# Freeing eight splits, moving the first weight sums behind block 1's routing, and adding an unread exponential

## The chip, the cores and the metric

The kernel runs on one core of a Trainium2 chip. The metric is device time in microseconds (us); lower is better. The engines are TensorE (PE, with its weight loads as PEld), VectorE (DVE), ScalarE (ACT), GpSimd (POOL) and SyncE (SP), which here only issues transfers. Each has its own queue of instructions and they meet through semaphores.

## The reference

Three stages follow one another: an attention with two local masks, a gated layer, and a soft mixture of experts. Cut to what matters here:

```python
attn_out = _attn_ref(q, k, v)                     # 4 x 8 x 576 x 64
x = attn_out.transpose(0, 2, 1, 3).reshape(2304, 512)
gate = 1.0 / (1.0 + np.exp(-(x @ w_gate)))        # w_gate, w_val: 512 x 1536
x = (gate * (x @ w_val)) @ w_out                  # w_out: 1536 x 512
logits = x @ phi                                  # 2304 x 32
d = softmax(logits, axis=0); c = softmax(logits, axis=1)
slot_input = d.T @ x                              # 32 slots, 4 for each of 8 experts
h = np.maximum(slot_input[e] @ w1[e], 0.0); slot_out[e] = h @ w2[e]
out = c @ slot_out
```

## The kernel before

The 2304 tokens are cut into five blocks: blocks 0 to 3 have 512 tokens, block 4 has 256. The work around the change is the passage from block 1 to the pair of blocks 2 and 3.

**Block 1** (`l1`, called for twelve column groups f of the gated layer) makes two groups of twelve matmuls for each f, one for the gate (ScalarE applies the sigmoid, L537) and one for the value (VectorE multiplies, L539). Every fp32 operand is split into a high part, a cast on ScalarE, and a low part, a subtraction. Between the groups, other work is put in: the attention scores, their transposes (tile `tr`, copied by ScalarE to `pt_ring`, L189), the weighted sums (`xp`, L208) of the blocks to come, and the routing of block 0.

**The routing** of a block is class `Post`: `logits` (PSUM tile `lt_ps`, then a running maximum and two exponentials on ScalarE, L805 and L809), twelve `turn` steps (four PE transposes each into a tile `tp`, copied to `gt` by ScalarE at L826 or VectorE at L824), `weights` (`dt_ps`) and three `gather` products (`sp`, added to `acc`, L862 and L864). For block 1 all copies to `gt` are ScalarE's.

**The pair** of blocks 2 and 3 (`pair_l1`, twelve f) uses a scheme of seven products of 2 by 2 blocks in place of eight. It wants differences of the tokens: `pair_sums` makes four of them on POOL (tile `tsum`, eight instructions at L577, steps 0 to 3 of two halves each). `pair_t` splits them into `t1` (from step 0), `t2` (step 2), `t3` (step 1) and `t4` (step 3): eight casts on ScalarE at L553 and eight subtractions on VectorE at L554 (tile `t_hl`). `pair_x2` and `pair_x3` split the tokens themselves (`b_hi`, `b_lo`, `b22`). It also wants sums of the weights of each f (class `PairW`, tile `s`, made by VectorE at L613) and their splits: `high0`, `high1`, `high2` are casts on ScalarE (L627, L630/L631, L641), `low0` is VectorE's, `low1` and `low2` are POOL's. `first_w`, `first_sums` and `first_splits` do that for f = 0. The products are at L651: `pa` (PSUM of the first, second, third and the last, in turn), `pd` and `pe`.

**What sets the order.** A scheduler places every instruction by its own estimate of times, except those given to `keep_in_program_order` (by `kept`, or by `kp` while `fixed[0]` is set; the helper `pinned` sets it around a call): these stay in the order in which they are written. Before the change all of `pair_sums` and `pair_t` are pinned and written ahead of block 1's routing, and `first_sums` and `first_splits` are the last two of the steps that `Spread` deals out between the routing's steps. PSUM tiles `tr`, `tp`, `pd` and `pe` share four banks (pool `ps_a`): the transposes of a new tile wait until the tile that had the bank is copied out. `xp`, `sp` and `lt_ps` share two (`ps_m`).

Of the kernel before, what the change touches and what calls it, by code (L numbers as in the profile page):

```python
# [7 lines left out]
F32 = mybir.dt.float32  # L8
# [4 lines left out]
AF = mybir.ActivationFunctionType  # L13
# [4 lines left out]
P = 128  # L18
# [4 lines left out]
NF = 12  # L23
# [32 lines left out]
def pb_tokens(n):  # L56
    return 512 if n < 4 else 256
# [3 lines left out]
def tile_kernel(  # L61
# [10 lines left out]
    nc = tc.nc  # L72

    cpool = ctx.enter_context(tc.tile_pool(name="cpool", bufs=1))
# [12 lines left out]
    def b8(tag, shape, dt, name):  # L87
        return big.tile(shape, dt, tag=tag, name=name, bufs=BUFS[tag])
# [28 lines left out]
    for i in range(SMALL):  # L117
        g = slice(32 * (i % 4), 32 * (i % 4) + 32)
# [392 lines left out]

    g_sb = {}
    g_cur = {}

    def l1(n, f, whl, between):
        nt = pb_tokens(n)
        per = 2048 // nt
        tag = {0: "ga", 1: "gb", 4: "xt" if f < per else "xb"}[n]
        if (n, f // per) not in g_cur:
            g_cur[n, f // per] = b8(tag, [P, per, nt], F32, "g")  # L520
        g = g_cur[n, f // per][:, f % per]
        for a in range(2):
            pt = ps_l1.tile([P, 512], F32, tag="l1", name="l1ps")
            first = True
            for dc in HP_ORDER:
                for w_, x_ in ((0, x_hi), (0, x_lo), (1, x_hi)):
                    nc.tensor.matmul(  # L527
                        pt[:, 0:nt],
                        lhsT=whl[:, w_, a, dc, :],
                        rhs=x_[n][:, dc, :],  # L530
                        start=first,
                        stop=(dc == HP_ORDER[-1] and w_ == 1),
                    )
                    first = False
            with tc.high_priority(offset=HIP):
                if a == 0:
                    nc.scalar.activation(g, pt[:, 0:nt], AF.Sigmoid)  # L537
                else:
                    nc.vector.tensor_tensor(g, pt[:, 0:nt], g, ALU.mult)  # L539
            between()  # L540
        g_sb[n, f] = g
# [10 lines left out]
    def split(eng, hi, lo, src_):  # L552
        kp(nc.scalar.copy(hi, src_))  # L553
        kp(eng.tensor_tensor(lo, src_, hi.bitcast(F32), ALU.subtract))  # L554
# [31 lines left out]
    def pair_t(z, c):  # L586
        name, at = (("t1", (0, 0)), ("t2", (2, 0)), ("t3", (0, 1)), ("t4", (2, 1)))[z]
        if c == 0:
            t = b8(("qk", "v")[z % 2], [P, 2, 2, 512], F32R, "t_hl")
            pair[name] = t[:, 0], t[:, 1]  # L590
        hi, lo = pair[name]
        split(nc.vector, hi[:, c], lo[:, c], pair["t", at[0]][:, at[1], c])
# [380 lines left out]
    for f in range(NF):  # L973
        whl = split_w(conv.pop(f), SPL)
        ahead(f + LA)
        if f >= 10:
            store()
            load_w(f - 10)
        l1(0, f, whl, sab if f < wo_first else ticking)
        if f in wo_at:  # L980
            convert(NF + wo_at[f])
# [10 lines left out]
    for f in range(NF):  # L992
        whl = split_w(wst[f // 2][:, f % 2])
        if f % 2:
            load_w(f // 2 + 2)
        l1(1, f, whl, beside)
        if NF + f in wo_at:
            convert(NF + wo_at[NF + f])
# [21 lines left out]
        prev_w[0].high2()  # L1020
        prev_w[0].low2()

    early_prep = [(pair_sums, z) for z in range(4)] + [(pair_t, z, c) for z in range(4) for c in range(2)]
    prep = [(pair_x2, z) for z in range(4)]
    prep += [(first_w,), (pair_x3, 0), (pair_x3, 1), (first_sums,), (first_splits,)]

    def pinned(fn, *args):
        fixed[0] = True
        fn(*args)
        fixed[0] = False  # L1030

    for x in early_prep:
        pinned(*x)
    prep = [(pinned, *x) for x in prep]
    after = after[mix0.done :] + Post(1).all()
    mix = Spread(prep, [(len(after) - 3, len(prep))])
    for fn, *args in after:
        fn(*args)
        mix()
    prev = None  # L1040
    w4 = []

# [26 lines left out]
    for f in range(NF):  # L1069
        l1(4, f, split_w(w4[f // 2][:, f % 2]), mix)  # L1070
        if f % 2:
            load_w4()
        for n, tags in ((n2, ["ga"] * 3), (len(after), ["gb"] * 3 + ["l2"] * 2)):
            if done < n <= mix.done:
                room += tags
                load_e(len(room))
        done = mix.done
        if f == NF - 2:
            load_wo("ws")
# [20 lines left out]
    for f in range(NF):  # L1100
        c = f % 4
# [18 lines left out]
    for e in range(8):  # L1120
        for h in range(2):
# [8 lines left out]
            tag = reuse.pop(0) if reuse else None  # L1130
# [226 lines left out]
```

## Time and profile before

| | us |
|---|---|
| median of three runs | 498.23 (497.89 to 499.33) |
| profiled execution, its own time | 498.77 |
| span of its core | 496.8 |
| PE busy | 470.1 (95%) |
| DVE busy | 301.4 (61%) |
| ACT busy | 248.6 (50%) |
| POOL busy | 158.3 (32%) |

The span is what the trace covers; 2 us of the execution lie around it. A row of the timeline has the start in us from the span's start, the duration, the engine, the line and the operation, the tile written and those read, the shape and the count; in brackets stands how long the engine was idle before and what released it. A row with a count merges neighbours, and rows of different engines, or of PE's overlapping matmuls, can overlap. Ends of matmuls are modelled.

### The profile page before, as it was taken

Reading aid. Unit: us, or ns where it says so; the run is one execution under the profiler, and the core shown is the slowest. Engines: PE = TensorE matmul, PEld = TensorE weight load, DVE = VectorE, ACT = ScalarE, POOL = GpSimd, SP = SyncE. Lnnn points to the kernel's source line nnn. Section 1 sums busy time; section 2 is a strip of 40 time slices with the busy share of each in tenths; the row PEclk is TensorE's granted clock in tenths of the full one; section 3 lists DMA queues with packets and bytes.
Section 4 is the critical chain, followed back from the end, with each engine's and each line's share of the span. In section 5 each row is a group of like instructions: output and inputs, shape, how many; then the busy total and the mean of one; then the engine's idle time right before and its main releaser. Section 6 shows DMA issues by size and latency. Waiting matters only on the chain.

```text
span 496.8 us, 12732 instructions
## 1 busy us (share of the span) xinstructions
PE 470.1 (95%) x5476; PEld 357.7 (72%) x5476; DVE 301.4 (61%) x561; ACT 248.6 (50%) x428; POOL 158.3 (32%) x132
## 2 busy tenths in 40 slices
PE   6789999999899999999889999999999999999993
PEld 3468877878677877877458888888887889643552
DVE  3969698967767353555956566556557665521522
ACT  2466566747666453546855545545435544300232
POOL 0243555635383321182143243342312134010100
PEclk9989999999999999999989999999999999989998
DMA  8979898979986501750020220220699795679997
GB/s 327 405 258 335 290 369 305 322 270 364 408 289 211 172 3 49 253 195 3 0 84 2 84 86 1 86 84 0 239 383 424 288 341 191 251 257 367 421 392 219
DMA packets 23784, 112.13 MB, mean 226 GB/s; under 512 B 2352, under 2 KB 7216, under 8 KB 14640
## 3 DMA queue, kind: packets, MB, share of 16 engines
q1 hardware_dynamic: 23408, 111.06, 60.1%
q8 instruction: 43, 0.70, 0.6%
q10 hardware_dynamic: 320, 0.26, 0.2%
q14 instruction: 13, 0.11, 0.1%
HBM read 97.16 MB, written 14.16 MB: 224 GB/s over the span
## 4 chain that ended last, share of the span: by engine, by line
PE 76%; DVE 3%; ACT 3%; issue 2%; DMA 1%; POOL 1%; SPq 0%; ACTq 0%; DVEq 0%; POOLq 0%
PE l1ps L527 27%; PE pa L651 13%; PE pe L651 6%; PE tp L821 4%; PE h_ps L1123 3%; PE pd L651 3%; PE xp L208 3%; PE so_ps L1182 2%; PE sp L852 2%; PE lt_ps L785 2%; PE s_ps L145 2%; PE wt_ps L468 1%; PE tr L188 1%; PE op L1221 1%; PE si_ps L1102 1%
## 5 line engine op out<-in xcount | busy, mean ns | idle before, releaser
L527 PE MATMUL l1ps<-x_hi,whl 128*128 128x512 f32 x384 | 129.5, 404 | 3.1 <-ACT x_hi L229 2.3
L527 PEld LDWEIGHTS l1ps<-x_hi,whl 128*128 128x128 f32 x384 | 72.2, 189 | 20.4 <-ACT x_hi L229 3.0
L527 PE MATMUL l1ps<-x_lo,whl 128*128 128x512 f32 x192 | 76.1, 397 | 0.0
L442 POOL TENSOR_TENSOR fw<-fw 128x512 int32<-128x512 int32 x36 | 51.4, 1437 | 71.5 <-DVE fw L441 35.1
L527 PEld LDWEIGHTS l1ps<-x_lo,whl 128*128 128x128 f32 x192 | 36.4, 190 | 7.2 <-issue 0.4
L539 DVE TENSOR_TENSOR g<-l1ps,g 128x512 f32<-128x512 f32 (+1 forms) x36 | 21.6, 600 | 32.7 <-PE l1ps L527 32.2
L527 PE MATMUL l1ps<-x,whl 128*128 128x256 f32 x288 | 37.2, 286 | 0.0
L527 PEld LDWEIGHTS l1ps<-x,whl 128*128 128x128 f32 x288 | 35.4, 191 | 2.1 <-issue 1.9
L537 ACT ACTIVATE g<-l1ps 128x512 f32<-128x512 f32 (+1 forms) x36 | 18.9, 526 | 30.2 <-PE l1ps L527 30.1
L494 POOL TENSOR_TENSOR whl<-w,whl 128x512 fp32r<-128x512 f32 x12 | 15.9, 1326 | 52.1 <-ACT whl L493 40.6
L821 PE MATMUL tp<-cst,g 128*128 128x128 f32 x216 | 28.6, 275 | 0.0
L494 POOL TENSOR_TENSOR whl<-wst,whl 128x512 fp32r<-128x512 f32 x12 | 16.1, 1340 | 38.6 <-ACT whl L493 33.9
L439 ACT ACTIVATE fw<-st 128x512 f32<-128x512 f32 x36 | 22.7, 675 | 10.9 <-DMA st<-wd 10.9
L821 PEld LDWEIGHTS tp<-cst,g 128*128 128x128 f32 x216 | 24.1, 140 | 3.6 <-ACT g L537 1.7
L494 DVE TENSOR_TENSOR whl<-fw,whl 128x512 fp32r<-128x512 f32 x24 | 22.0, 922 | 5.8 <-ACT whl L493 5.3
L720 DVE TENSOR_TENSOR tm<-pe,tm 128x512 f32<-128x512 f32 x12 | 8.3, 692 | 27.7 <-PE pe L651 27.7
L826 ACT COPY gt<-tp 128x512 f32<-128x512 f32 x33 | 18.5, 587 | 10.9 <-PE tp L821 9.3
L441 DVE TENSOR_SCALAR fw<-st 128x512 int32<-128x512 uint32 x36 | 22.6, 654 | 1.9 <-DMA st<-wd 1.9
L208 PEld LDWEIGHTS xp<-pt_ring,v 64*64 64x64 f32 x1216 | 19.2, 135 | 6.1 <-issue 4.0
L493 ACT CAST whl<-fw 128x512 fp32r<-128x512 f32 x24 | 14.7, 619 | 17.3 <-POOL fw L442 13.2
L440 DVE TENSOR_SCALAR fw<-fw 128x512 uint32<-128x512 uint32 x36 | 20.7, 584 | 2.7 <-ACT fw L439 2.2
L208 PE MATMUL xp<-pt_ring,v 64*64 64x32 f32 (+1 forms) x1216 | 20.7, 219 | 1.6 <-issue 0.9
(464 smaller groups left out, 961.2 us busy)
## 6 DMA issues: line engine op xcount, KB each, us to landing
ew<-w SPq DMA_DIRECT2D x32, 1024.0 KB, 7.9
st<-wd SPq DMA_DIRECT2D x18, 1024.0 KB, 9.0
wst<-wg SPq DMA_DIRECT2D x12, 1024.0 KB, 6.9
v<-qkv SPq DMA_DIRECT2D x20, 512.0 KB, 6.7
wg<-fw SPq DMA_DIRECT2D x12, 512.0 KB, 7.7
w<-wg SPq DMA_DIRECT2D x6, 1024.0 KB, 7.4
qk<-qkv SPq DMA_DIRECT2D x10, 576.0 KB, 6.4
qk<-qkv SPq DMA_DIRECT2D x8, 528.0 KB, 5.5
```

Of the source, the lines that this page charges most:

```text
L208: nc.tensor.matmul(o, lhsT=v[k, t, i, r, :], rhs=p_[k, 2 * r + t, i, 0:nq], start=True, stop=True)
L439: nc.scalar.activation(top, st[:, c, 1].bitcast(F32), AF.Prelu, scale=2.0**-112, alpha=2.0**32)
L440: nc.vector.tensor_scalar(top.bitcast(U32), top.bitcast(U32), 3, None, ALU.logical_shift_left)
L441: nc.vector.tensor_scalar(low.bitcast(I32), st[:, c, 0], 2.0**-29, None, ALU.mult)
L442: nc.gpsimd.tensor_tensor(low.bitcast(I32), top.bitcast(I32), low.bitcast(I32), ALU.add)
L494: (nc.gpsimd if pool[h] else nc.vector).tensor_tensor(whl[:, 1, h], src[:, h], whl[:, 0, h].bitcast(F32), ALU.subtract)
L527: nc.tensor.matmul(pt[:, 0:nt], lhsT=whl[:, w_, a, dc, :], rhs=x_[n][:, dc, :], start=first, stop=(dc == HP_ORDER[-1] and w_ == 1),)
L537: nc.scalar.activation(g, pt[:, 0:nt], AF.Sigmoid)
L539: nc.vector.tensor_tensor(g, pt[:, 0:nt], g, ALU.mult)
L651: nc.tensor.matmul(pt, lhsT=w[:, w_, P * c : P * c + P], rhs=x_[:, c], start=first and c == 0 and w_ == 0 and x_ is hi, stop=c == 1 and w_ ...
L821: nc.tensor.transpose(tp[:, c], g_sb[self.n, 4 * q + c][:, P * j : P * j + P], ident)
L826: nc.scalar.copy(to, tp)
```

## The change

Three edits. `pair_t` is no longer pinned: its sixteen instructions may be placed by the scheduler. `first_sums` and `first_splits` are taken out of the dealt steps and written, pinned, behind the whole routing of block 1. And behind block 1's last sigmoid ScalarE takes an exponential of one column into a tile `unread` that nothing reads. The later lines move by 1 to 7 (L553 becomes L556, L826 becomes L829).

```diff
+    unread = cpool.tile([P, 1], F32, tag="unread", name="unread")
...
                 if a == 0:
                     nc.scalar.activation(g, pt[:, 0:nt], AF.Sigmoid)
+                    if n == 1 and f == NF - 1:
+                        nc.scalar.activation(unread, g[:, 0:1], AF.Exp)
...
-    early_prep = [(pair_sums, z) for z in range(4)] + [(pair_t, z, c) for z in range(4) for c in range(2)]
     prep = [(pair_x2, z) for z in range(4)]
-    prep += [(first_w,), (pair_x3, 0), (pair_x3, 1), (first_sums,), (first_splits,)]
+    prep += [(first_w,), (pair_x3, 0), (pair_x3, 1)]
...
-    for x in early_prep:
-        pinned(*x)
+    for z in range(4):
+        pinned(pair_sums, z)
+    for z in range(4):
+        for c in range(2):
+            pair_t(z, c)
...
     for fn, *args in after:
         fn(*args)
         mix()
+    pinned(first_sums)
+    pinned(first_splits)
```

The order on POOL and SP stays as it was, and so does everything up to block 1's last column group and from the pair's second f on. ScalarE's queue at the end of block 1, before (l1ps_3035 and l1ps_3105 are the gate groups of f = 10 and 11):

```order
L537 ACTIVATE g_2706<-l1ps_3035 128x512
L826 COPY gt_3017<-tp_3055 128x512
L189 COPY pt_ring_90<-tr_3081 128x512
L826 COPY gt_3087<-tp_3094 128x512
L537 ACTIVATE g_2706<-l1ps_3105 128x512
L189 COPY pt_ring_90<-tr_3119 128x512
L826 COPY gt_3087<-tp_3131 128x512
```

The same place after the change, where every name's number is one or two higher; t_hl_3239 is `t2`, from the step-2 difference tsum_3229, and t_hl_3234 is `t1`:

```order
L538 ACTIVATE g_2707<-l1ps_3036 128x512
L829 COPY gt_3018<-tp_3056 128x512
L556 CAST t_hl_3239<-tsum_3229 128x512 x2
L189 COPY pt_ring_90<-tr_3082 128x512
L556 CAST t_hl_3234<-tsum_3224 128x512
L829 COPY gt_3088<-tp_3095 128x512
L556 CAST t_hl_3234<-tsum_3224 128x512
L538 ACTIVATE g_2707<-l1ps_3106 128x512
L189 COPY pt_ring_90<-tr_3121 128x512
L540 ACT_TABLE_LOAD
L540 ACTIVATE unread_173<-g_2707 128x1
L829 COPY gt_3088<-tp_3133 128x512
```

Four of the eight casts now stand ahead of the last sigmoid, the two of `t2` ahead of the copy of the transposed scores.

VectorE's queue at the same place, before (l1ps_3067 and l1ps_3137 are the value groups of f = 10 and 11; all eight subtractions of `pair_t` stood further down, behind the copies of the next two `sp` to `acc`):

```order
L862 COPY acc_77<-sp_3061 128x512
L539 TENSOR_TENSOR g_2706<-l1ps_3067,g_2706 128x512
L824 COPY gt_3087<-tp_3088 128x512
L824 COPY gt_3087<-tp_3125 128x512
L539 TENSOR_TENSOR g_2706<-l1ps_3137,g_2706 128x512
```

And after:

```order
L865 COPY acc_77<-sp_3062 128x512
L557 TENSOR_TENSOR t_hl_3239<-tsum_3229,t_hl_3239 128x512 x2
L542 TENSOR_TENSOR g_2707<-l1ps_3068,g_2707 128x512
L827 COPY gt_3088<-tp_3089 128x512
L557 TENSOR_TENSOR t_hl_3234<-tsum_3224,t_hl_3234 128x512 x2
L827 COPY gt_3088<-tp_3127 128x512
L557 TENSOR_TENSOR t_hl_3244<-tsum_3224,t_hl_3244 128x512 x2
L542 TENSOR_TENSOR g_2707<-l1ps_3139,g_2707 128x512
```

The two subtractions of `t2` stand ahead of a multiplication and a copy of block 1, and only those of `t4` stay behind the last multiplication.

ScalarE's queue where the pair begins, before (s_3405 holds the weight sums, w1__3365 and w2__3366 the splits of f = 0, w1__3466 one of f = 1, tm_3455 the pair's partial sums):

```order
L631 CAST w1__3365<-s_3405 128x256
L631 CAST w1__3466<-s_3405 128x256
L641 CAST w2__3366<-s_3405 128x768
L711 COPY tm_3455<-pe_3458 128x512
L703 ACT_TABLE_LOAD
L703 ACTIVATE g_3453<-tm_3455 128x512
```

And after:

```order
L634 CAST w1__3380<-s_3444 128x256
L706 ACT_TABLE_LOAD
L706 ACTIVATE g_3455<-tm_3457 128x512
L644 CAST w2__3381<-s_3444 128x768
L634 CAST w1__3468<-s_3444 128x256
L714 COPY tm_3457<-pe_3460 128x512
```

The table load and the pair's first sigmoid now precede the 768-wide cast (`high2` of f = 0).

## Rows read from the trace of the kernel before

**Rows 1.** The page, its first line.

```profile
span 496.8 us, 12732 instructions
```

**Rows 2.** PE's waits from 218 to 275 us: total, times, longest.

```profile
PE pe L651 <- ACT w__3365 L631: 2.0, 1, 2.0
PE dt_ps L831 <- ACT d L809: 0.9, 1, 0.9
PE c_ps L880 <- DVE lt L793: 0.6, 1, 0.6
PE pa L651 <- POOL w__3366 L613: 0.4, 1, 0.4
```

**Rows 3.** Timeline of PE, 218 to 272 us.

```profile
223.47 1.04 PE L821 MATMUL tp<-cst,g 128*128 128x128 f32 x8
224.26 0.48 PE L527 MATMUL l1ps<-x_hi,whl 128*128 128x512 f32 x1
...
227.19 1.59 PE L208 MATMUL xp<-pt_ring,v 64*64 64x32 f32 x96
...
231.61 2.83 PE L785 MATMUL lt_ps<-g,wp 128*32 128x128 f32 x96
...
249.96 2.90 PE L651 MATMUL pe<-t_hl,w__3365 128*128 128x512 f32 x6 [2.03 <-ACT w__3365 L631]
...
254.69 1.19 PE L651 MATMUL pa<-t_hl,w__3366 128*128 128x512 f32 x4 [0.43 <-POOL w__3366 L613]
...
258.06 0.39 PE L651 MATMUL pa<-b_hi,w__3466 128*128 128x512 f32 x1
...
262.14 1.52 PE L651 MATMUL pe<-t_hl,w__3466 128*128 128x512 f32 x6
```

**Rows 4.** Timeline of ScalarE, 218 to 272 us.

```profile
219.59 0.59 ACT L189 COPY pt_ring<-tr 128x512 f32<-128x512 f32 x1 [3.80 <-PE tr L188]
...
229.37 4.26 ACT L553 CAST t_hl<-tsum 128x512 fp32r<-128x512 f32 x8
...
238.17 1.28 ACT L805 ACT_TABLE_LOAD   x1
239.47 0.20 ACT L805 ACTIVATE nm<-nm 128x1 f32<-128x1 f32 x1
...
245.55 1.14 ACT L553 CAST b<-xf 128x512 fp32r<-128x512 f32 x2 [1.45 <-DVE b_lo L554]
246.60 0.40 ACT L630 CAST w__3365<-wst 128x256 fp32r<-128x256 f32 x1
...
251.72 0.83 ACT L641 CAST w__3366<-s 128x768 fp32r<-128x768 f32 x1 [1.48 <-DVE s L613]
```

**Rows 5.** Timeline of VectorE, 218 to 272 us.

```profile
219.22 0.69 DVE L539 TENSOR_TENSOR g<-l1ps,g 128x512 f32<-128x512 f32 x1 [2.30 <-PE l1ps L527]
...
232.33 4.89 DVE L554 TENSOR_TENSOR t_hl<-tsum,t_hl 128x512 fp32r<-128x512 f32 x8
237.15 0.28 DVE L793 COPY lt<-lt_ps 128x128 f32<-128x128 f32 x1
...
249.05 0.75 DVE L613 TENSOR_TENSOR s<-wst 128x256 f32<-128x256 f32 x2
```

**Rows 6.** Timeline of POOL, 218 to 272 us.

```profile
217.92 3.78 POOL L577 TENSOR_TENSOR tsum<-xf 128x512 f32<-128x512 f32 x3
221.66 5.02 POOL L577 TENSOR_TENSOR tsum<-xf,tsum 128x512 f32<-128x512 f32 x4
...
252.62 2.02 POOL L613 TENSOR_TENSOR w__3366<-s,w__3366 128x768 fp32r<-128x768 f32 x1 [1.90 <-ACT w__3366 L641]
```

**Rows 7.** Timeline of all engines, 199.5 to 202.5 us.

```profile
200.89 0.59 ACT L189 COPY pt_ring<-tr 128x512 f32<-128x512 f32 x1 [1.58 <-PE tr L188]
...
201.53 0.42 PEld L821 LDWEIGHTS tp<-cst,g 128*128 128x128 f32 x4 [0.32 <-ACT pt_ring L189]
```

**Rows 8.** Half-microsecond stretches: busy time by engine, granted clock (1.00 full), DMA.

```profile
250.00:250.50 0.50, 0.50 (x2) 0.39 (x2) 0.50 (x2) 0.24 (x1) 0.50 (x1) 0.56 0.00 0
...
253.00:253.50 0.50, 0.50 (x2) 0.10 (x1) 0.00 (x0) 0.48 (x2) 0.50 (x1) 0.53 0.00 0
```

## The prediction

> **What bounds the kernel now.** PE works through nearly the whole span of 496.8 us [rows 1], so I asked where it waits at the place that the change touches, and then read the queues of the other engines for the cause. PE's waits between 218 and 275 us add up to 4 us [rows 2]. In the order of time: for `lt` on VectorE (0.6), for the exponential `d` on ScalarE (0.9), for the cast of the first weight sum (2.0) and for POOL's `low2` (0.4). Two causes are plain. VectorE copies `lt` only at 237.15, straight behind eight splits of 4.89 us [rows 5], while the logits end near 231.61 + 2.83 = 234.4 [rows 3]. ScalarE loads a table at 238.17 for 1.28 us ahead of the exponentials [rows 4]. The last mark is the pair's second f, which PE begins at 258.06 [rows 3]; behind it both orders are the same, so what the change is worth is how far this mark moves.
>
> **The wait that the change adds.** The scheduler now puts the casts of `t2` first. They read the step-2 difference, and on POOL its two halves are the first two of the four from 221.66 on, 5.02 / 4 = 1.26 us apart [rows 6]: they end near 222.95 and 224.2. Nothing that stands ahead of them on POOL has changed. So ScalarE, which had been idle for 3.80 us until 219.59 [rows 4], stands at the first cast until 223.0, casts, stands again until 224.25, casts until 224.85 (a cast takes 4.26 / 8 = 0.53, or 0.6 to its end), and only then copies the transposed scores to `pt_ring`, until 225.4 in place of 220.2. What is queued behind: that copy, a `gt` copy, the last sigmoid. Who waits: the second transposes after a `tr` need a bank of `ps_a`. That such a bank is given free by the `pt_ring` copy is seen twenty microseconds earlier, where weight loads of `tp` waited 0.32 for it [rows 7]. Here the next `tp` ran at 223.47 [rows 3]; it now starts at 225.4, 1.95 later.
>
> VectorE does the same again: the subtractions of `t2` wait for the casts and end at 225.5 (4.89 / 8 = 0.61 each), then come the multiplication that stood at 219.22 [rows 5] and the copy of a `tp`, until 226.8. The second `tp` of PE's pair needs that copy's bank, so it starts at 226.85, and block 1's last twelve matmuls at 227.3 in place of 224.26 [rows 3]. **The first term is +3.0 us** of PE standing still.
>
> That later instructions do not pass a waiting one on ScalarE is seen in the rows: the cast of 245.55 waited 1.45 for `b_lo`, and the next instruction, a cast of weights that needs nothing of it, ran only at 246.60 [rows 4]. [...]
>
> **What is given back.** From the last l1 group to the logits PE had 224.26 to 231.61, or 7.35 [rows 3]. Now there are four transposes more ahead (half of the eight of 223.47, 0.4) and about 0.4 of waiting, since the unread exponential's load (1.28, at 228) and the casts of `t3` (1.1) push ScalarE's casts of the last `xp` from 230.9, when these are ready, to 231.7. The logits then begin at 235.2 and end at 238.0. VectorE is free by then, as its splits are done, and copies `lt` at 238.1 in place of 237.15 [rows 5]: of the 3.0 us all but 0.95 is back.
>
> From there to the first weight sum, at 249.05 [rows 5], it was 11.9 us. The load is off this path, but the cast and copy that the scheduler put ahead of `d` fill its place (`d` at 240.5; before, right behind the exponential of 239.47 [rows 4]). What now sets the pace is ScalarE itself: from the copy that ends its wait for the logits (238.6) to the last `gt` copy stand 14 copies and casts of 0.53, three small ones (0.5) and one wait for `b_lo` (0.75), together 8.7, and I get 247.3. The last gather follows (until 248.4), VectorE's addition to `acc`, and only then, since `first_sums` is pinned behind the routing, the first sum: 249.2, 0.15 later than before. **The second term is -2.85 us.**
>
> **The start of the pair.** From the first sum: its cast (249.7 to 250.05), then the table load that now stands ahead of `high2` (to 251.35), the sigmoid (to 251.9), `high2` at 251.9 against 251.72 [rows 4], `low2` on POOL for 2.02 [rows 6] until 254.8, against 254.64. Behind that, PE had 14 products left from 254.69 to 258.06 [rows 3], as two of `b22`'s stood ahead of the wait; now 16 are left, 16 x 0.23 = 3.65. The second f begins at 258.5. **The third term is +0.3**, and the three make +0.45 us at the full clock. The casts and the load that changed place cost nothing more: the same eight casts, the same eight subtractions, the same two loads (238.17 has become 228) and one exponential of one column, bounded by the 0.20 of the one at 239.47 [rows 4].
>
> [...]
>
> **The clock.** [...] A fall as long as the one in the rows costs up to 3.4 / 2 = 1.7; part of it may lie in the wait. From 0 to 1.7, I take 1.1, near the upper end as the wait is the longer. The second: near 249 to 254.8 PE waits 1.1, 0.3, 0.9 and 1.6 with few products between, and 16 products behind it have no cover; again 0 to 1.7, where before it cost next to nothing. I take half, 0.85. **The fourth term is +1.95.**
>
> **The sum.** 3.0 - 2.85 + 0.3 + 1.95 = +2.4 us. The profiled execution would take 498.77 + 2.4 = 501.2; it lay 0.54 above the median of the runs, and on the median the change gives 498.23 + 2.4 = **500.6 us**.
>
> **The rivals.** *No wait, so faster.* If POOL's step-2 difference were there by 219.6, the transposed scores would be copied on time, the first term would fall away, and the earlier `lt` copy would carry through: with every mark 3.0 earlier and the same pace behind it the second f would begin near 255.5, that is 495.6 us. It decides at the time that POOL ends the fifth difference; the rows put that at 222.95, with POOL at work without a gap since 217.92 [rows 6], and I see nothing that would move it by 3 us. Chance 0.1. *The wait without the clock.* If PE's clock does not fall, or falls where it is covered, +0.45 is left: 498.7, no change that can be seen. For it speaks that a fall can lie in a wait, as the one of before mostly did [rows 8]; against it, that the new wait is longer than the one ahead of that fall [rows 3]. Chance 0.17. *The clock falls twice, in full.* 0.45 + 1.7 + 1.7 = +3.85, or 502.1. Chance 0.15. *The change doesn't do what it says*, that is, the moved load and splits leave the second f where it was, is the second rival by its number. The forecast (one fall or two partial ones, 499.7 to 501.6) has 0.58.
>
> **How the numbers follow.** A difference of 0.3%, 1.5 us, is about what a measurement of this kernel can tell from no change; the bounds are 496.7 and 499.7. Faster: the first rival but for 0.01, 0.09. Within: that 0.01, the second rival (0.17) and the lower edge of the forecast (0.07), 0.25. Slower: 0.66, the rest of the forecast (0.51) and the third rival (0.15). The range leaves out the first rival (0.1) and the upper half of the third (0.07): 498.2 to 502.0.
>
> **What would show it.** In the profile of the changed kernel ScalarE idles some 7 us before the first `t_hl` cast, released by POOL; PE waits near 223.4 for `pt_ring`, 2 us, and near 226 for VectorE, 1 us; `lt` is copied about 1 us later than 237.15 with no splits ahead of it; the first sum stands at 249 to 251, behind the last addition to `acc`; the stretch behind 226 shows the lower clock. If the first cast of `t2` starts before 220, or PE shows no wait at `tp`, the first term is wrong; if the granted clock is full from 225 to 260, the fourth is.

## The result, and the profile after

| | before | after | ratio, 95% interval |
|---|---|---|---|
| median of eight runs each, on one chip | 497.86 us | 501.87 us | 1.0073 (1.0047 to 1.0098) |
| the same change again, beside the experiments | 497.89 us (27 runs) | 503.09 us (6 runs) | 1.0100 (1.0056 to 1.0144) |
| span of the profiled execution | 496.8 us [rows 1] | 503.1 us | |

The change makes the kernel slower, by 4.0 us in the first comparison of medians and 5.2 in the second (3.6 and 5.0 by the ratios), where 2.4 were forecast. 501.87 lies inside the range (498.2 to 502.0), at its upper end; the median of the repeat lies above it. One execution of run e2 below (508.89 us, at a mean granted clock of 0.972) fell in a slower state of the chip and is left out of its median and ratio.

The profiled execution of after is the slowest of its eight (505.17 us), and part of that is not the change: its granted clock stands at 0.50 of full from 131 to 134 us, in a stretch that the change does not touch and where the execution of before has 1.00, and by block 1's last transposed scores (`tr`) it is already 3.4 us late. So both traces are read from the last `tr` on: it begins at 223.04 in before and at 226.47 in after, and from there to the pair's second f there are 35.02 us (to 258.06 [rows 3]) and 39.65 us (to 266.12). The repeat, whose trace has no such delay, has 40.00.

What PE waits for after the change, between 215 and 280 us (total, times, longest), in place of [rows 2]:

```profile
PE tp L824 <- DVE gt L827: 1.6, 1, 1.6
PE tp L824 <- ACT pt_ring L189: 1.5, 1, 1.5
PE pa L654 <- POOL w__3381 L616: 1.2, 1, 1.2
PE pe L654 <- ACT w__3380 L634: 0.8, 1, 0.8
PE pa L654 <- ACT w__3381 L644: 0.6, 1, 0.6
```

The waits for `lt` and for `d` are gone; two at `tp` have come. These `tp` are transposes of block 0's routing, which run between block 1's last two groups of matmuls. The timeline of PE, against [rows 3] (start, length, engine, line, operation, count, the wait in front and who ended it):

```profile
226.47 0.60 PE L188 MATMUL tr<-cst,qk 128*128 128x128 f32 x4
228.61 0.66 PE L824 MATMUL tp<-cst,g 128*128 128x128 f32 x4 [1.54 <-ACT pt_ring L189]
230.90 1.12 PE L824 MATMUL tp<-cst,g 128*128 128x128 f32 x4 [1.64 <-DVE gt L827]
231.67 0.78 PE L528 MATMUL l1ps<-x_hi,whl 128*128 128x512 f32 x1
...
236.97 1.59 PE L208 MATMUL xp<-pt_ring,v 64*64 64x32 f32 x96
...
262.36 1.19 PE L654 MATMUL pa<-t_hl,w__3381 128*128 128x512 f32 x4 [1.16 <-POOL w__3381 L616]
...
266.12 0.39 PE L654 MATMUL pa<-b_hi,w__3468 128*128 128x512 f32 x1
```

The eight transposes that ran in one piece at 223.47 now stand in two, with a wait in front of each, and block 1's last twelve matmuls (the value group of f = 11) take 5.30 us (231.67 to 236.97) in place of 2.93. ScalarE, against [rows 4], shows why the first wait is there:

```profile
226.21 0.62 ACT L556 CAST t_hl<-tsum 128x512 fp32r<-128x512 f32 x1 [7.01 <-POOL tsum L580]
227.45 0.62 ACT L556 CAST t_hl<-tsum 128x512 fp32r<-128x512 f32 x1 [0.62 <-POOL tsum L580]
227.97 0.58 ACT L189 COPY pt_ring<-tr 128x512 f32<-128x512 f32 x1
...
231.07 1.28 ACT L540 ACT_TABLE_LOAD   x1
232.36 0.20 ACT L540 ACTIVATE unread<-g 128x1 f32<-128x1 f32 x1
...
257.11 0.40 ACT L634 CAST w__3380<-s 128x256 fp32r<-128x256 f32 x1 [0.99 <-DVE s L616]
257.54 1.28 ACT L706 ACT_TABLE_LOAD   x1
258.83 0.63 ACT L706 ACTIVATE g<-tm 128x512 f32<-128x512 f32 x1
259.58 0.83 ACT L644 CAST w__3381<-s 128x768 fp32r<-128x768 f32 x1
```

It idles 7 us, until POOL has step 2, with the copy of the scores behind the casts. VectorE and POOL, against [rows 5, 6]:

```profile
226.86 2.79 DVE L557 TENSOR_TENSOR t_hl<-tsum,t_hl 128x512 fp32r<-128x512 f32 x2 [6.53 <-ACT t_hl L556]
...
230.17 0.67 DVE L827 COPY gt<-tp 128x512 f32<-128x512 f32 x1
...
244.84 0.29 DVE L796 COPY lt<-lt_ps 128x128 f32<-128x128 f32 x1 [2.55 <-PE lt_ps L788]
...
256.66 0.42 DVE L616 TENSOR_TENSOR s<-wst 128x256 f32<-128x256 f32 x1
```

```profile
219.92 5.01 POOL L580 TENSOR_TENSOR tsum<-xf 128x512 f32<-128x512 f32 x4
224.89 5.88 POOL L580 TENSOR_TENSOR tsum<-xf,tsum 128x512 f32<-128x512 f32 x4
```

`lt` is now copied as soon as the logits are there; nothing stands ahead of it. The two subtractions of `t2` take 2.79 us, where eight of them took 4.89 in before. One-microsecond stretches (length, busy time by engine, granted clock, DMA), against [rows 8], give the third thing: the lower level of the clock, 0.50 of full, from inside the second wait on.

```profile
230.00:231.00 1.00, 0.10 (x1) 0.10 (x2) 1.00 (x3) 1.00 (x3) 0.78 (x1) 0.50 0.00 0
...
236.00:237.00 1.00, 1.00 (x7) 0.36 (x5) 0.00 (x0) 0.00 (x0) 0.00 (x0) 0.61 0.00 0
```

### The profile page after: what moved, and what is told of

The parts are those of the page before. It is cut to its first block, busy times and chain, and to the rows that moved or that the text cites. A ratio compares the mean times of both kernels' runs of the same rounds, so it can differ in the third digit from the quotient of the medians.

```text
span 503.1 us, 12730 instructions
## 1 busy us (share of the span) xinstructions
PE 471.0 (94%) x5476; PEld 358.5 (71%) x5476; DVE 305.5 (61%) x561; ACT 248.0 (49%) x429; POOL 159.3 (32%) x132
## 4 chain that ended last, share of the span: by engine, by line
PE 73%; POOL 3%; ACT 3%; DVE 3%; DMA 3%; issue 2%; SPq 0%; DVEq 0%; ACTq 0%
PE l1ps L528 25%; PE pa L654 13%; PE pe L654 6%; PE tp L824 4%; PE pd L654 3%; PE h_ps L1130 3%; PE sp L855 3%; PE so_ps L1189 2%; PE xp L208 2%; PE lt_ps L788 2%; PE s_ps L145 2%; POOL tsum L580 1%; DMA v<-qkv 1%; PE wt_ps L468 1%; PE tr L188 1%
## 5 line engine op out<-in xcount | busy, mean ns | idle before, releaser
L528 PE MATMUL l1ps<-x_hi,whl 128*128 128x512 f32 x384 | 131.0, 408 | 3.5 <-ACT x_hi L229 2.6
L528 PEld LDWEIGHTS l1ps<-x_hi,whl 128*128 128x128 f32 x384 | 73.4, 192 | 21.2 <-ACT x_hi L229 3.3
L824 PE MATMUL tp<-cst,g 128*128 128x128 f32 x216 | 30.4, 279 | 3.7 <-DVE gt L827 1.6
L829 ACT COPY gt<-tp 128x512 f32<-128x512 f32 x33 | 18.7, 585 | 12.9 <-PE tp L824 10.8
L145 PE MATMUL s_ps<-qk 64*32 64x64 f32 x1280 | 16.7, 229 | 6.5 <-DMA qk<-qkv 3.9
```

The lines of the kernel that those rows point to most:

```text
L145: return nc.tensor.matmul(to, lhsT=u["qk"][d, 128 * t + 32 * i : 128 * t + 32 * i + 32], rhs=u["qk"][d, 512 + o : 512 + o + 64], start=Fal ...
L528: nc.tensor.matmul(pt[:, 0:nt], lhsT=whl[:, w_, a, dc, :], rhs=x_[n][:, dc, :], start=first, stop=(dc == HP_ORDER[-1] and w_ == 1),)
L824: nc.tensor.transpose(tp[:, c], g_sb[self.n, 4 * q + c][:, P * j : P * j + P], ident)
L829: nc.scalar.copy(to, tp)
```

## The experiments

The theory: ScalarE's casts of `t2` wait for POOL's step 2 with the copy to `pt_ring` behind them, PE stands still at `tp`, and its clock falls there; the second and third part of the change by themselves cost little. The rivals: the loss lies in the later sums or the moved load, or in the work of the splits rather than in the wait, or the clock falls there anyway.

All runs in one table. Each ratio is to executions of before that were taken beside the run. The four columns of distances are start times in each trace, in us from block 1's last `tr`, to block 1's last group of matmuls (`l1`), the copy of `lt`, the first weight sum and the second f; the last column says whether the granted clock was at its lower level, 0.50 of full, in between: for 3.4 us where it says once, 3.4 each time where it says twice, 6.8 where it says long.

| kernel | median us | ratio to before (95%) | `l1` | `lt` | sum | second f | low clock |
|---|---|---|---|---|---|---|---|
| before | | | 1.22 | 14.11 | 26.01 | 35.02 | once |
| after | 501.87 | 1.0073 (1.0047 to 1.0098) | 5.20 | 18.37 | 30.19 | 39.65 | long, at `l1` |
| after again (e4) | 503.09 | 1.0100 (1.0056 to 1.0144) | 5.20 | 17.12 | 28.92 | 40.00 | twice |
| first part alone (e2) | 501.73 | 1.0073 (1.0043 to 1.0103) | 5.32 | 18.55 | 30.27 | 40.53 | long, at `l1` |
| second part alone (e7) | 497.28 | 0.9995 (0.9974 to 1.0015) | 1.23 | 14.11 | 25.60 | 34.88 | once |
| third part alone (e6) | 495.56 | 0.9966 (0.9941 to 0.9991) | 1.23 | 14.13 | 23.42 | 33.05 | none |
| second and third (e1) | 498.63 | 1.0016 (0.9990 to 1.0041) | 1.23 | 14.13 | 25.75 | 36.47 | long, at the sums |
| e1, `high2` first (e12) | 497.16 | 0.9985 (0.9957 to 1.0013) | 1.23 | 14.13 | 25.74 | 34.23 | none |
| after, t1 and t3 first (e3) | 496.82 | 0.9960 (0.9935 to 0.9986) | 1.22 | 13.05 | 22.93 | 32.75 | none |
| e3, sums mixed in (e8) | 495.06 | 0.9945 (0.9921 to 0.9969) | 1.23 | 13.18 | 22.41 | 31.99 | none |
| e8, a split later (e11) | 497.35 | 0.9988 (0.9966 to 1.0011) | 1.23 | 13.04 | 22.25 | 33.33 | once |
| after, step 2 early (e5) | 498.63 | 1.0014 (0.9990 to 1.0038) | 2.50 | 13.59 | 25.42 | 36.48 | once, at the end |
| e5 without steps 1, 3 (e10) | 496.74 | 0.9990 (0.9956 to 1.0023) | 1.68 | 12.49 | 24.29 | 33.75 | none |
| after, the wait filled (e9) | 501.76 | 1.0057 (1.0025 to 1.0088) | 4.88 | 15.68 | 27.48 | 36.93 | none |

### Which part loses: e2, e1, e4

The first part alone, against before:

```diff
-    for x in early_prep:
-        pinned(*x)
+    for z in range(4):
+        pinned(pair_sums, z)
+    for z in range(4):
+        for c in range(2):
+            pair_t(z, c)
```

> The first part of the change alone: the splits may move, the weight sums stay among block 1's routing, no unread exponential. The theory expects the same two waits of PE at block 1's `tp` (1.5 to 2 and 1 to 1.6 us), the lower clock behind them, and a time 2 to 5 us above before (500 to 503). The rival, that the other two parts carry the loss, expects no more than before and perhaps less (495.5 to 498), since the earlier copy of `lt` would be a gain.

It is all of the loss: +3.8 us by the medians (3.6 by the ratio), with PE's waits at `tp` of 1.67 and 1.64 us and the lower clock behind them (0.50 from 228 to 233). The rest of the change, against after:

```diff
-            pair_t(z, c)
+            pinned(pair_t, z, c)
```

> The change without its first part: the splits of the token differences keep their written place, the first weight sums stay behind block 1's routing and the unread exponential stays behind the last sigmoid. If the loss comes from the casts that wait for POOL ahead of the copy of the transposed scores (the theory), PE's two waits at block 1's `tp` (1.5 for `pt_ring`, 1.6 for `gt`) are gone, the clock is full from 226 to 237, `lt` is copied near 237.2 as before, and the time is that of before within 1.5 us (497 to 499.5). If the loss comes from the other two parts (the later sums, or the load that then stands ahead of `high2`), the time is still 500.5 or more and the waits at `tp` are not needed for it.

Without the first part the waits at `tp` are gone (`l1` 1.23 behind `tr`, 1.22 in before) and the time is that of before within the interval, as the theory had it. What it did not have is in the last columns: the second f lies 1.45 us later than in before. That is taken up below.

> The changed kernel once more, beside the others on the same chip. If the early delay of its profiled execution (some 3.5 us at 131 to 134 us, ahead of all that the change touches) was one of that execution alone, this profile lies some 1 to 4 us lower, near 500.7 to 502.5, and shows again the two waits at `tp`, 3 us in sum, and the lower clock right behind them; if the clock fell there by chance, the stretch from 226 to 237 is at the full clock this time.

The two waits are there to the hundredth (1.54 and 1.64). The time is above the 500.7 to 502.5 expected (503.37 for the profiled execution). The clock is not the same as in the first execution: a short fall at `l1`, to 0.50 for 3.4 us, back at full for the last of its matmuls, and another one of that size at the start of the pair (stretches as above):

```profile
231.00:232.00 1.00, 1.00 (x4) 0.77 (x3) 0.47 (x1) 1.00 (x2) 0.00 (x0) 0.50 0.00 0
232.00:234.00 2.00, 2.00 (x32) 1.42 (x31) 1.06 (x3) 0.02 (x1) 0.00 (x0) 1.00 0.00 0
259.00:260.00 1.00, 0.96 (x3) 0.77 (x4) 0.97 (x2) 0.00 (x0) 1.00 (x2) 0.65 0.00 0
```

### The wait for POOL: e3, e5

In e3 only t1 and t3, which read steps 0 and 1, may move:

```diff
-    for z in range(4):
+    for z in (0, 2):
         for c in range(2):
             pair_t(z, c)
+    for z in (1, 3):
+        for c in range(2):
+            pinned(pair_t, z, c)
```

> The change, with one difference: of the token differences only t1 and t3 are free to move (they read POOL's steps 0 and 1, which end by 221.7), while t2 and t4, which read steps 2 and 3, keep a written place behind them. The theory says that what costs is the wait for step 2 alone: ScalarE copies the transposed scores to `pt_ring` by 221 to 222, PE's wait at `tp` for it is under 0.5 us, the clock does not fall behind it, and the time is 495.5 to 498. The rival, that it is the work of splits ahead of block 1's end that costs, or a clock that falls there in any case, expects 500 or more.

ScalarE now copies the scores before any cast:

```profile
221.49 0.58 ACT L189 COPY pt_ring<-tr 128x512 f32<-128x512 f32 x1 [3.84 <-PE tr L188]
221.97 0.62 ACT L556 CAST t_hl<-tsum 128x512 fp32r<-128x512 f32 x1
```

PE has no wait at `tp`, the clock stays full (1.00 from 215 to 262), and the kernel is faster than before, by 1.1 us by the medians and 2.0 by the ratio (0.7 to 3.2). The marks move the way the prediction's first rival had it: `lt` 1.06 us earlier (2.05 by the rival's sum), the first sum 3.08 (2.85), the second f 2.27 (2.56). But e3 holds the change's other two parts as well, and the unread exponential alone is worth 2.0 (e6, below). What freeing t1 and t3 gives is read from pairs that differ in that alone: e3 beside e1 has 1.8 us by the medians (2.8 by the ratios, intervals apart), e8 beside e6 0.5 (1.0, intervals overlapping).

e5 leaves after's order alone on every engine but POOL:

```diff
-    for z in range(4):
+    for z in (0, 2, 1, 3):
         pinned(pair_sums, z)
```

> The changed kernel with one line different: POOL takes its four differences in the order 0, 2, 1, 3, so that step 2 stands where step 1 stood, 2.5 us earlier; every other engine keeps its instructions in the order of the changed kernel. The theory (ScalarE stands at t2's casts until POOL has step 2) expects PE's two waits at `tp`, 3.1 us in sum, to shrink to 0.6 or less, a full clock behind them, and a time of 496 to 498. The rival, that the work of t2's casts and subtractions ahead of the copies is what delays PE, expects the waits to stay over 2 us and the time over 500, since that work is all still there.

It gives back most of the loss, though not all that the theory expected (498.63 against 496 to 498), and shows that the wait for step 2 was only one of two. The wait for `pt_ring` is gone; the one for VectorE stays over the 0.6 expected, and now stands alone:

```profile
227.77 0.66 PE L824 MATMUL tp<-cst,g 128*128 128x128 f32 x4 [1.06 <-DVE gt L827]
```

### VectorE beside POOL: e10

The durations of VectorE's eight subtractions (minimum, median, maximum in ns; first and last start), in before and in e5:

```profile
L554 DVE TENSOR_TENSOR t_hl<-tsum,t_hl x8: 681/682/685, 232.3 to 236.5; 128x512 fp32r<-128x512 f32 x8
```

```profile
L557 DVE TENSOR_TENSOR t_hl<-tsum,t_hl x8: 676/898/1800, 223.7 to 234.7; 128x512 fp32r<-128x512 f32 x8
```

In before they ran after POOL had ended (226.7 [rows 6]); in e5 the first four run beside POOL's differences, and POOL's become longer too:

```profile
L580 POOL TENSOR_TENSOR tsum<-xf x4: 1282/1507/1745, 219.2 to 225.9; 128x512 f32<-128x512 f32 x4
```

e10 takes POOL's later differences away and leaves all else where it is (t3 and t4 are then split from differences 0 and 2 as well; the other two are left out of the computation):

```diff
-    for z in (0, 2, 1, 3):
+    for z in (0, 2):
         pinned(pair_sums, z)
-("t3", (0, 1)), ("t4", (2, 1))
+("t3", (0, 0)), ("t4", (2, 0))
```

> The version with POOL's order 0, 2, 1, 3, without steps 1 and 3: POOL takes only the differences 0 and 2, and t3 and t4 are split from these in their place, so that part of what is computed is left out. ScalarE, VectorE and PE keep their instructions in the same order. If VectorE's subtractions are long there because POOL takes differences at the same time (theory: 1.4 to 1.8 us for one beside POOL, 0.68 alone), the second and later ones take 0.68, PE's remaining wait of 1.1 us for VectorE's `gt` copy falls under 0.4 us, and the time is 0.7 to 2 us under that version (496.6 to 498). If they are long for another cause (where their operands lie, or the casts that run beside them), they stay at 1.2 us or more, the wait stays and so does the time, 498 to 499.

```profile
L557 DVE TENSOR_TENSOR t_hl<-tsum,t_hl x8: 679/688/1120, 222.1 to 232.1; 128x512 fp32r<-128x512 f32 x8
```

```profile
225.32 0.66 PE L824 MATMUL tp<-cst,g 128*128 128x128 f32 x4 [0.24 <-DVE gt L827]
```

All but the first subtraction, which still meets POOL's last difference, are back at 0.68 us, the wait falls from 1.06 to 0.24, and the time by 1.9 us by the medians (1.2 by the ratios, whose intervals overlap; e5's trace also has a fall of the clock at the end, to 0.50 from 257 to 260.5, which e10's has not). So the second wait at `tp` comes from POOL as well, by slowing VectorE. Both grow longer: in e5 two subtractions took 2.83 us in place of 1.28 (1.55 more, near the 1.26 of one difference), and POOL's two beside them 3.42 in place of 2.54 (0.88 more, near the 0.61 to 0.68 of one subtraction). Taken one by one, the two subtractions end at 224.80 and 226.51, each 0.55 behind the end of the POOL instruction that was at work when they began (224.25 and 225.96). By what means the two engines hold each other up, no run shows.

### The clock: e9

Twelve products that nobody reads, six ahead of each waiting transpose:

```diff
+            if self.n == 0 and q == 2 and j >= 2:
+                fill = ps_m.tile([P, 512], F32, tag="m", name="fill")
+                for _ in range(6):
+                    nc.tensor.matmul(fill, lhsT=msk[:, M_ID:M_COLS], rhs=msk[:, 0:512], ...)
             tp = pool.tile([P, 4, P], F32, tag=tag, name="tp")
```

> The changed kernel with twelve more products on PE that nobody reads, in a bank of their own: six ahead of each of the two transposes that wait at `tp`, so that PE works in the place where it waited (the gt copy behind the load also falls behind two casts on ScalarE, nothing else moves). Theory: the lower clock behind the wait, which made block 1's last twelve matmuls 5.3 us long in place of 2.9, comes from PE standing still there; with the wait filled the granted clock stays full from 226 to 237, the second f comes 1.5 to 2.5 us earlier, and the time is 499 to 501 where the changed kernel has 501.9 to 503.1. Rival: the fall comes there whatever PE does in the 3 us, so the clock is at its lower level again, and the time is 502 or more.

```profile
226.68 0.66 PE L828 MATMUL tp<-cst,g 128*128 128x128 f32 x4 [0.28 <-ACT pt_ring L189]
227.18 1.46 PE L824 MATMUL fill<-msk 128*128 128x512 bf16 x6
228.98 0.65 PE L828 MATMUL tp<-cst,g 128*128 128x128 f32 x4 [0.34 <-DVE gt L831]
...
261.44 0.39 PE L654 MATMUL pa<-b_hi,w__3482 128*128 128x512 f32 x1
```

```profile
226.00:232.00 6.00, 5.38 (x28) 3.54 (x26) 5.40 (x9) 5.97 (x12) 2.86 (x2) 1.00 0.00 0
232.00:262.00 30.00, 26.62 (x323) 17.23 (x322) 21.98 (x45) 19.73 (x40) 8.00 (x7) 1.00 0.07 21
```

In its trace the forecast of the theory came out: the clock is full throughout (1.00 from 226 to 262), block 1's last twelve matmuls take 2.92 us again, and the second f comes 36.93 us behind `tr` in place of 39.65 and 40.00, with all else of after in place but one `gt` copy, which falls behind two casts on ScalarE. The median did not follow: 501.76, and 1.0057 of before where after has 1.0073 and 1.0100, with intervals that overlap. The twelve executions lie between 498.55 and 503.07, five at 498.6 to 500.4 (the profiled one is the highest of these) and seven at 501.6 and more, while no execution of after lies below 500.68. The mean granted clock of each execution points to a lower clock in the seven: 0.984 on average, against 0.989 in the five (0.983 and 0.982 over the executions of after and of its repeat). Where in the span it fell is not known, so this stays open. Shown is what a full clock is worth in one execution, not that the filling keeps it.

### The start of the pair: e7, e6, e12

> The second part alone: the pair's first weight sums behind all of block 1's routing. The theory has it near nothing: the first sum comes later than before by 0.2 to 1 us, the pair's second f by 0.3 to 1 us, the time is 497.5 to 499.4. The rival, that this part carries a large share of the loss, expects 500 or more and a second f 2 us or more later against block 1's last gate matmuls.

Second part alone (`first_sums` and `first_splits` behind the loop, `t` and the load as in before): nothing that can be told, by the time and by the trace. The first sum comes 0.4 us and the second f 0.14 us earlier, where the theory had both 0.2 to 1 later.

> The third part alone: the unread exponential behind the last sigmoid, all splits and weight sums where they were. The theory says that the load leaves the stretch ahead of `d`, so that PE's wait for `d` (0.9) falls under 0.5 us, but the last weight split still waits for the first sums; 496.8 to 498.6, no difference that can be told. The rival, that a table load beside block 1's last copies costs PE, expects waits at `tp` or `xp` of over 0.5 us and 499 or more.

Third part alone (the exponential line, nothing else): 2.0 us faster by the median and by the trace (1.7 by the ratio), which neither side expected. The wait for `d` hardly changed (0.9 to 0.7). What changed is the order that the scheduler made behind it: VectorE's first sum stands between the additions to `acc`, ahead of the second f's split, 2.6 us earlier than in before, the cast of it is there in time, and PE's wait of 2.03 us with its clock fall [rows 3, 8] does not come up (1.00 from 248 to 257):

```profile
246.45 0.41 DVE L616 TENSOR_TENSOR s<-wst 128x256 f32<-128x256 f32 x1
246.78 0.74 DVE L867 SCALAR_TENSOR_TENSOR acc<-acc,nm,sp 128x512 f32<-128x512 f32 x1
```

With the second part added (e1), the sums go behind again, and the table load goes ahead of the casts that wait for them:

```profile
248.24 1.28 ACT L706 ACT_TABLE_LOAD   x1
249.53 0.63 ACT L706 ACTIVATE g<-tm 128x512 f32<-128x512 f32 x1
250.07 0.39 ACT L634 CAST w__3380<-s 128x256 fp32r<-128x256 f32 x1
```

```profile
250.51 3.39 PE L654 MATMUL pe<-t_hl,w__3380 128*128 128x512 f32 x6 [2.56 <-ACT w__3380 L634]
```

e12 pins the pair's first sigmoid, with its load, behind `high2`:

```diff
-        kp(nc.scalar.activation(g2, m1, AF.Sigmoid))
+        (kept if f == 0 else kp)(nc.scalar.activation(g2, m1, AF.Sigmoid))
```

> The second and third parts of the change (that run: 498.6, where the third alone has 495.6), with the pair's first sigmoid and its table load pinned behind `high2` on ScalarE; two of `b22`'s products then stand ahead of the wait again, and VectorE and POOL keep their order. If the load in front of the casts of the sums is what the later sums cost, PE's wait of 2.6 us for the first of these casts falls to 1.8 or less, the clock falls later or not at all, and the time is 495.5 to 497.8. If the later sums cost by VectorE's order alone (the addition to `acc` behind a wait for ScalarE's `tm`), the time stays at 498 to 499.

```profile
250.47 2.02 PE L654 MATMUL pe<-t_hl,w__3380 128*128 128x512 f32 x6 [1.69 <-ACT w__3380 L634]
```

The wait falls by 0.87 us, the clock stays full (1.00 from 250 to 258, where e1 has 0.50 from 251 to 255), and the second f is 2.24 us nearer in the trace. The medians differ by 1.5 us with intervals that overlap; the trace is the evidence here, one execution of each.

### The best version: e8, e11

e8 is e3 with the sums back in the routing's list (`prep += [..., (first_sums,), (first_splits,)]`, the two lines behind the loop gone).

> As the version in which only t1 and t3 may move, but with the first weight sums back among block 1's routing. If the gain of that version (about 1 us under before, second f some 2 us nearer to block 1's last gate matmuls) comes from the earlier `lt` alone, the time is the same or up to 0.7 us better, 495.8 to 497.3. If the later sums carry the gain, because VectorE then adds to `acc` sooner, the time goes back to before, 497.3 to 498.5.

At 495.06 us it is 0.55% faster than before (0.31 to 0.79%), the lowest of all, though the intervals of e3 and e6 overlap with its own; the earlier `lt` is kept, and the first sum comes another 0.5 us earlier. The step from e3 is 0.75 us by the ratios and 0.76 in the traces (the medians differ by 1.8). The time lies below both ranges expected (495.8 was the lower end for the earlier `lt` alone), so whether the place of the sums adds to the gain is not settled; it does not carry it, since with the sums late e3 gains already.

e11 moves the second f's weight split of 0.68 us behind its sums (`high0` and `low0` at f = 0 where the other f have them).

> The fastest version so far (t1 and t3 free, unread exponential, first sums among the routing), with the pair's second weight split moved behind its sums, as the later f have it: 0.68 us of VectorE leave the place ahead of the sums that `high2` waits for. If those sums pace the start of the pair, `high2`'s cast and PE's wait for it come 0.3 to 0.7 us earlier and the time is 494.3 to 495; if the copy of `pe` ahead of it on ScalarE paces it, nothing changes, 495 to 495.5; if the split then comes too late for the second f, PE shows a new wait near 257 and the time is 495.5 or more.

It failed. `high2`'s cast comes 0.1 us earlier and PE waits the same 1.4 us for it, since the cast stands right behind the copy of `pe` on ScalarE in both; the split, now beside POOL's `low2`, takes 2.31 us, and in PE's next wait the clock falls (0.70 from 252 to 253, 0.50 from 253 to 255):

```profile
252.64 2.08 PE L654 MATMUL pa<-t_hl,w__3368 128*128 128x512 f32 x4 [0.77 <-POOL w__3368 L616]
```

The same four products take 1.19 in e8, with a wait of 0.73:

```profile
253.02 1.19 PE L654 MATMUL pa<-t_hl,w__3368 128*128 128x512 f32 x4 [0.73 <-POOL w__3368 L616]
```

Why the clock falls in one and not in the other is not settled.

## Why the prediction was right, and where it was short

**The mechanism** is as forecast: the cast that stands ahead of the copy, the two waits of PE, most of the delay regained by `lt` (at full clock, in e9, `lt` is 1.57 later than in before; 0.95 were worked out), the clock. The step that decided against the rival "no wait" was reading POOL's end of step 2 from its row of four; e3, where the scores are copied on time for another reason, gave 2.27 us in the trace where the rival had 2.6 in its sum. That the number fell inside the range is in part luck: it did so by 0.13 us, and the repeat of the same change lies 1.1 above.

**The first term** (+3.0): at full clock e9 gives 3.66 (4.88 less 1.22). Its first half was right: the first `tp` 2.14 us behind `tr` in after, 2.36 worked out. The second half was short by 0.6: the second `tp` 4.43 behind `tr`, 3.81 worked out. The mis-sized item is the duration of the subtraction, taken as 0.61 us from eight that ran with POOL idle [rows 5, 6], for a place where POOL was at work; e10, with POOL out of the way, has `l1` 1.68 behind `tr`, e5 2.50.

**The second term** (-2.85): from `l1` to the logits the prediction's marks have 7.9 us, and e9 has 7.90. That agreement is luck: the items named (7.35, 0.4 and 0.4) add up to 8.15, and in e9 the 0.4 of waiting does not come (ScalarE idles 1.78 ahead of the casts of the last `xp`), while the four transposes more cost 0.55. From there to the copy of `lt` 2.9 were worked out, and e9 has 2.90. From `lt` to the first sum 11.1 were worked out, and e9 has 11.80, after 11.82. The mis-sized item is the wait for `b_lo`, put at 0.75; in after it is 1.45, as it had been in before [rows 4]:

```profile
251.42 0.62 ACT L556 CAST b<-xf 128x512 fp32r<-128x512 f32 x1 [1.45 <-DVE b_lo L557]
```

So 0.7 us less came back than was forecast.

**The third term** (+0.3): from the first sum to the second f 9.01 us in before, 9.46 in after and 9.45 in e9: +0.44. What the prediction put at nothing is the load that leaves the path from `lt` to the first sum, since a cast and a copy fill its place. In after that holds, with the sums pinned behind the routing. By itself (e6) the move has the first sum 2.6 us earlier and the time 2.0 lower.

The three make +0.45 by the prediction, and +1.91 in e9 (36.93 less 35.02): this, 0.6 and 0.7 above all, is most of what the forecast lacked.

**The fourth term** (+1.95, one fall of 1.1 and one of 0.85) is an estimate from the one fall in the trace of before: behind PE's wait of 2.03 us the granted clock stood at 0.50 of full for 3.4 us, 0.56 and 0.53 in the first and last half-microsecond [rows 8], and six products took 2.90 us in place of 1.52 [rows 3]. No run shows 1.95. The runs show 2.7 us in after (39.65 less 36.93), in one long stretch at `l1`; 3.1 in the repeat, where the first fall cost 1.12 (`l1` 4.04 us long in place of 2.92) and the second 1.63 (11.08 from the sum to the second f in place of 9.45). The places were right, the cause as far as the traces go, and the sizes low: a fall was taken to last 3.4 us, as in [rows 8], and the one in after lasted 6.8. Which of the two forms comes differs from execution to execution. Of the fourteen traces the clock falls at `l1` in the three that have both waits (after, e4, e2) and in none of the others; that filling the waits keeps it full is shown in one trace only.

**The table load** costs its own 1.28 us here: the activation behind it begins 0.01 us after its end (231.07 + 1.28 = 232.35 and 232.36), and 0.02 after it in before [rows 4].

## What to carry to other kernels

Before work is set free to move, look at who produces its input and when: here the splits of `t2`, whose input came late, put ahead of a copy that was ready, cost 3.6 to 5.2 us, and freeing only t1 and t3, whose input was ready, cost nothing and won 0.5 to 1.8 by the medians. Where VectorE and POOL work on such differences at the same time, price each at its time beside the other (in e5 up to 1.80 us in place of 0.68, and 1.75 in place of 1.28). And read the order that a scheduler makes of each part alone: a part that was costed at nothing gave 2 us by itself and lost them in company.

## What had not been expected of the hardware

A VectorE subtraction of 128x512 takes 0.68 us with POOL idle (before) and up to 1.80 beside POOL's subtractions (e5), and POOL's go from 1.28 (e10) to 1.75 (e5). In the pair's start the same is seen at 128x256, where in after one sum takes 0.41 us and the next, with POOL at work, 2.06:

```profile
260.08 0.41 DVE L616 TENSOR_TENSOR s<-wst 128x256 f32<-128x256 f32 x1
260.52 2.06 DVE L616 TENSOR_TENSOR s<-s,wst 128x256 f32<-128x256 f32 x1
```

Nor do the executions of one program agree on where the granted clock falls: in after's trace it is at 0.50 of full at `l1` for 6.8 us, in e4's, the same kernel, there for 3.4 and again at the start of the pair, and such a place moved the second f by 1.1 to 2.7 us.
